# Zero products in front of the turns and products of the query columns, and one fixed PSUM place for them

## Chip, core and metric

One NeuronCore of a Trainium2 chip runs the whole program. The metric is the device time of one execution in microseconds; lower is better. The kernel before was timed three times: median 1874.4 us (1872.93 to 1878.34).

## What is computed

The reference chains three parts: a linear attention, a mixture of eight experts that sends each token to two of them, and a second feed-forward part with a cosine gate. Cut to its core:

```python
q_s = softmax(q over head_dim); k_s = softmax(k over seq)       # (8, 8, 576, 64)
kv  = einsum('bhsd,bhse->bhde', k_s, v)
x   = einsum('bhsd,bhde->bhse', q_s, kv)  -> (4608, 512)
noisy = x @ w_gate + log1p(exp(x @ w_noise)) * noise
top2 experts of each token, weights from a softmax over the two
out[token] += weight * (relu(x[token] @ w1[e]) @ w2[e])
h = out @ w_in ; result = (h * cos(h)) @ w_out
```

## The kernel before

The 4608 tokens are 36 *columns* of 128 tokens: nine for each of four pairs of batches, the ninth of a pair being the last 64 tokens of both.

- **Attention.** 16 steps `s` (batch, half of the heads) load k and v and run `k_stage` (the maximum over the sequence, turned on TensorE, subtracted on GpSimd at L293, exponential on ScalarE at L295) and `kv_stage` (products into `pkv`, L316). Between them stand the query columns.
- **A query column** is `x_unit(n)`: `x_t(n + 1)` turns the queries of the column after it (four transposes, L371, into `pqt`; ScalarE writes their exponential to `qtt`, L373), and `x_mm(n)` multiplies `qtt` with `KVN` into `px` (L387; L392 for a ninth column). VectorE then reads `px` four times: `dx` (L395), `xs` (L398), `lx` (L400), and sums `lx` into the gate logits `lg` (L401). SyncE stores `xs` to `x_d`. `px` is a tile of a PSUM pool with one buffer, so the products of a column wait until VectorE has read those of the column before. `pqt` and `qtt` have two buffers each.
- **Routing.** When columns 0 to 17 are done, `routing(0)` works out on VectorE which token goes to which expert (L444 to L546). Its last steps compare slots (`lo`, `eq`, `bl`, L429), multiply them on TensorE into `ptb` (L532) and write the token lists (`TB` L535, `rit` L539, `idx` L546). Columns 18 to 26 and 27 to 35 have a `routing` of their own.
- **Experts.** With the first lists, GpSimd gathers rows of `x_d` (L621), TensorE turns them (`pt`, L674) and the first three groups of expert 0 (`early_group`) run between the columns from 27 on: `mm1` (`ph`, L753 to L755) and `mm2` (`acc`, L777 to L779). After the columns come the other experts and the last part, over 80% of the time.

The order on each engine is not that of the source. The program is recorded under `schedule_with_timeline_sim=True`: a scheduler takes the recorded instructions and puts those of each engine in an order by its own estimate of their times, within the dependences. `tc.issue_after(x)` adds one dependence, that the instruction comes behind `x` on its engine. The weights of the experts are split on ScalarE and GpSimd (L139, L140) in between.

Of the kernel before, what the change touches and what calls it, by code (L numbers as in the profile page):

```python
# [10 lines left out]
F32 = mybir.dt.float32  # L11
F32R = mybir.dt.float32r
BF16 = mybir.dt.bfloat16
# [8 lines left out]
P = 128  # L22
# [5 lines left out]
def tile_attention_moe_moe2(  # L28
# [14 lines left out]
    nc = tc.nc  # L43
# [25 lines left out]
    consts = ctx.enter_context(tc.tile_pool(name="consts", bufs=1))  # L69
    psa = tc.alloc_tile_pool(name="psa", bufs=1, space=PSUM, side="right")  # L70
# [4 lines left out]
    def ps_at(name, tag, bufs):  # L75

        return psa.tile([P, 512], F32, name=name, tag=tag, bufs=bufs)
# [16 lines left out]
    flag = consts.tile([P, 1 + E], I32, name="flag")  # L94
    ident = consts.tile([P, P], F32, name="ident")
    make_identity(nc, ident)

    def w_pieces(e):

        if e < E:
            a, b = w1[e], w2[e]
        else:
            h = e - E
            a, b = wi_d[:, h * F:(h + 1) * F], wo_d[h * F:(h + 1) * F, :]
        res = []
        for fh in range(2):
            for kc in range(NK):  # L110
                res.append((0, kc, fh, a.rearrange("(p k) f -> k p f", k=NK)[kc, :, fh * 512:(fh + 1) * 512]))
            for f in range(4 * fh, 4 * fh + 4):
                res.append((1, f, 0, b[f * P:(f + 1) * P, :]))
        return res
# [69 lines left out]
    KVN = [at.tile([P, 4, 81], F32, name=f"kvn{i}") for i in range(B)]  # L184
# [172 lines left out]
        nc.gpsimd.tensor_tensor(ql, ql, qm[:, :, None].to_broadcast([P, H, D]), op=ALU.subtract)  # L357

    QTT = {}

    def x_t(n):

        t, c9 = divmod(n, PC)
        pt = ps_at("pqt", "tr", 2)
        for i in range(4):
            if c9 < 8:
                b, c = 2 * t + c9 // 4, c9 % 4
                src = QE[2 * b + i // 2][:, c, 2 * (i % 2):2 * (i % 2) + 2, :]
            else:
                src = QTL[t][:, 2 * i:2 * i + 2, :]  # L370
            nc.tensor.transpose(pt[:, i * P:(i + 1) * P], src.rearrange("p h d -> p (h d)"), ident)  # L371
        qtt = at.tile([P, 4, P], F32, name="qtt", bufs=2)
        behind.append(nc.scalar.activation(qtt, pt.rearrange("p (i s) -> p i s", i=4), AF.Exp))  # L373
        QTT[n] = qtt

    def x_mm(n):
        t, c9 = divmod(n, PC)
        qtt = QTT.pop(n)
        xs = at.tile([P, H, D], F32, name="xs", bufs=4)
        den = at.tile([P, 2, 4], F32, name="dx", bufs=3)  # L380
        px = psa.tile([P, 2, 512], F32, name="px", tag="px", bufs=1)
        for i in range(4):
            for r in range(2):
                rs = slice(64 * r, 64 * r + 64)
                o = px[:, r, i * 81:i * 81 + 81]
                if c9 < 8:
                    nc.tensor.matmul(o, qtt[rs, i, :], KVN[2 * t + c9 // 4][rs, i, :], start=True, stop=True,  # L387
                                     tile_position=(64 * r, 0))
                else:
                    for b2 in range(2):  # L390
                        ts = slice(64 * b2, 64 * b2 + 64)
                        nc.tensor.matmul(o[ts], qtt[rs, i, ts], KVN[2 * t + b2][rs, i, :], start=True, stop=True,  # L392
                                         tile_position=(64 * r, 64 * b2))
        pv = px[:, :, :324].rearrange("p r (i e) -> p r i e", i=4)
        nc.vector.tensor_single_scalar(den, pv[:, :, :, 64], EPS, op=ALU.add)  # L395
        nc.vector.reciprocal(den, den)
        xv = xs.rearrange("p (i r) d -> p r i d", r=2)
        nc.vector.tensor_tensor(xv, pv[:, :, :, :64], den[:, :, :, None].to_broadcast([P, 2, 4, 64]), op=ALU.mult)  # L398
        lx = at.tile([P, 2, 4, 2 * E], F32, name="lx", bufs=2)
        nc.vector.tensor_tensor(lx, pv[:, :, :, 65:], den[:, :, :, None].to_broadcast([P, 2, 4, 2 * E]), op=ALU.mult)  # L400
        nc.vector.tensor_reduce(LG[:, n, :], lx.rearrange("p r i g -> p g (r i)"), axis=AX.X, op=ALU.add)  # L401
        xf = xs.rearrange("p h d -> p (h d)")
        if c9 < 8:
            r0 = (2 * t + c9 // 4) * S
            dst = x_d[r0:r0 + SM, :].rearrange("(p c) m -> p c m", c=4)[:, c9 % 4, :]
            nc.sync.dma_start(dst, xf)
        else:
            for b2 in range(2):
                r0 = (2 * t + b2) * S + SM
                nc.sync.dma_start(x_d[r0:r0 + 64, :], xf[64 * b2:64 * b2 + 64])  # L410
# [179 lines left out]
    def x_unit(n):  # L590
        if n == 0:
            x_t(n)
        if n + 1 < NCOL:
            x_t(n + 1)
        x_mm(n)
        for i, (_, c1) in enumerate(CHUNKS):
            if n + 1 == c1:
                bg.add(routing(i))
# [426 lines left out]
    for n in range(n, NCOL):  # L1025
        t, c9 = divmod(n, PC)
# [57 lines left out]
    with tc.If(over > 0):  # L1084
        with tc.tile_pool(name="gp", bufs=1, reuse_waits="tile") as gp:
            with tc.For_i(0, NT // P, 1) as blk:
# [17 lines left out]
                for e in range(E):  # L1104
# [5 lines left out]
                    for f in range(NF):  # L1110
                        ph = ps_tr("gph")
                        for kc in range(NK):
                            nc.tensor.matmul(ph[:, :P], wa_t[:, kc, f * P:(f + 1) * P], xt[:, kc, :],
                                             start=kc == 0, stop=kc == NK - 1)
# [6 lines left out]
                for h in range(2):  # L1121
# [4 lines left out]
                    for f in range(NF):  # L1126
                        ph = ps_tr("gph")[:, :P]
                        for kc in range(NK):
                            nc.tensor.matmul(ph, wa_t[:, kc, f * P:(f + 1) * P], xt[:, kc, :],
                                             start=kc == 0, stop=kc == NK - 1)  # L1130
                        kk = gp.tile([P, P], F32, name="gkk", bufs=2)
                        r = gp.tile([P, P], F32, name="gr", bufs=2)
                        times_cos(r, kk, ph)
                        nc.tensor.matmul(acc, r, wb_t[:, f, :], start=h == 0 and f == 0,
                                         stop=h == 1 and f == NF - 1)
# [34 lines left out]
```

## Time and profile before

| | |
|---|---|
| median of 3 runs | 1874.4 us (1872.93 to 1878.34) |
| profiled execution: its own time | 1874.38 us |
| its span, first to last instruction | 1872.4 us |
| TensorE busy | 1798.1 us (96%) |
| VectorE, ScalarE, GpSimd busy | 1136.9, 857.8, 452.4 us |
| mean granted TensorE clock | 0.968 of full speed |

The span lacks 2.0 us of the execution's time: what lies before the first and behind the last instruction. TensorE is written PE, its weight loads PEld, VectorE DVE, ScalarE ACT, GpSimd POOL, SyncE's queue SPq. The profile's *PEclk* is the TensorE clock that was granted: 1.00 is 2.4 GHz, 0.50 is 1.2 GHz.

### The profile page before, as it was taken

The numbers are of one execution on the slowest core, as the hardware profiler recorded it, in microseconds if no ns is written. First come the engines' busy times: TensorE is split into PE (matmuls) and PEld (weight loads), VectorE is DVE, ScalarE is ACT, GpSimd is POOL, SyncE is SP. The second block draws the span as 40 slices with busy tenths as digits, with TensorE's granted clock in tenths as the row PEclk, the third lists the DMA queues.
The fourth block names the chain that finished last, engine by engine and source line by source line (L and its number), as shares of the span: only waits on it lengthen the run. The fifth ranks groups of instructions, "written<-read, shape, count | busy, mean of one in ns | idle before, by whom it ended". The sixth has DMA issues, their size and how long they took to land. (4 is left out here: it accounts for less than half of the span.)

```text
span 1872.4 us, 27040 instructions
## 1 busy us (share of the span) xinstructions
PE 1798.1 (96%) x9738; PEld 1525.2 (81%) x9738; DVE 1136.9 (61%) x2138; ACT 857.8 (46%) x1514; POOL 452.4 (24%) x405
## 2 busy tenths in 40 slices
PE   5885999999999999999999999999999999999998
PEld 3674888898988889888888878888888888888886
DVE  4658653686757567575652466565656556565654
ACT  5542223332332323333232376666666666666654
POOL 5556125332313133231323262010101001010000
PEclk7875899999999999999999999999999999999999
DMA  9954335554535455354543352020302021211000
GB/s 265 290 170 121 102 103 189 178 167 142 182 109 161 136 157 173 103 166 130 160 136 111 118 157 68 23 84 7 90 7 84 18 74 29 63 40 40 1 23 24
DMA packets 179775, 206.19 MB, mean 110 GB/s; under 512 B 34224, under 2 KB 121264, under 8 KB 179632
## 3 DMA queue, kind: packets, MB, share of 16 engines
q1 hardware_dynamic: 160704, 152.17, 27.3%
q0 software_dynamic: 12160, 39.86, 7.4%
q10 hardware_dynamic: 6768, 12.32, 1.8%
q8 instruction: 82, 1.34, 0.3%
q14 instruction: 61, 0.50, 0.1%
HBM read 127.06 MB, written 49.43 MB: 94 GB/s over the span
## 5 line engine op out<-in xcount | busy, mean ns | idle before, releaser
L753 PE MATMUL ph<-xh,w1h 128*128 128x512 f32 (+2 forms) x1376 | 489.4, 356 | 3.1 <-DVE r L699 3.1
L755 PE MATMUL ph<-xh,w1l 128*128 128x512 f32 (+2 forms) x1376 | 489.0, 355 | 0.0
L754 PE MATMUL ph<-xl,w1h 128*128 128x512 f32 (+2 forms) x1376 | 488.9, 355 | 0.0
L777 PE MATMUL acc<-w2h,hh 128*128 128x512 f32 x1152 | 451.5, 392 | 1.9 <-ACT hh L765 1.3
L778 PE MATMUL acc<-w2l,hh 128*128 128x512 f32 x1152 | 450.2, 391 | 0.0
L779 PE MATMUL acc<-w2h,hl 128*128 128x512 f32 x1152 | 422.1, 391 | 0.6
L753 PEld LDWEIGHTS ph<-xh,w1h 128*128 128x128 f32 x1376 | 260.1, 189 | 41.0 <-DVE r L699 3.6
L754 PEld LDWEIGHTS ph<-xl,w1h 128*128 128x128 f32 x1376 | 260.1, 189 | 37.6 <-issue 0.8
L755 PEld LDWEIGHTS ph<-xh,w1l 128*128 128x128 f32 x1376 | 259.9, 189 | 31.9
L759 ACT ACTIVATE hh<-ph 128x256 fp32r<-128x256 f32 (+2 forms) x200 | 95.6, 478 | 392.2 <-PE ph L755 387.6
L760 DVE SCALAR_TENSOR_TENSOR hl<-ph,hh 128x256 fp32r<-128x256 f32 (+2 forms) x200 | 108.1, 541 | 247.0 <-ACT hh L759 238.7
L777 PEld LDWEIGHTS acc<-w2h,hh 128*128 128x128 f32 x1152 | 216.5, 188 | 47.6 <-ACT hh L765 3.3
L779 PEld LDWEIGHTS acc<-w2h,hl 128*128 128x128 f32 x1152 | 215.1, 188 | 46.1 <-issue 1.6
L778 PEld LDWEIGHTS acc<-w2l,hh 128*128 128x128 f32 x1152 | 216.5, 188 | 40.4
L699 DVE SCALAR_TENSOR_TENSOR r<-r,ph 128x512 f32<-128x512 f32 x144 | 98.9, 687 | 152.8 <-ACT r L698 152.1
L140 POOL TENSOR_TENSOR w1l<-wst,w1h 128x512 fp32r<-128x512 f32 x80 | 106.1, 1329 | 258.0 <-ACT w1h L139 241.5
L697 ACT ACTIVATE r<-r 128x512 f32<-128x512 f32 x144 | 90.6, 629 | 149.4 <-DVE r L696 149.3
L766 DVE TENSOR_TENSOR hl<-r,hh 128x512 fp32r<-128x512 f32 x144 | 100.5, 698 | 86.2 <-ACT hh L765 86.1
L140 POOL TENSOR_TENSOR w2l<-wst,w2h 128x512 fp32r<-128x512 f32 x80 | 106.6, 1337 | 134.2 <-ACT w2h L139 106.2
L621 POOL DMA_INDIRECT xg<-y_d,SL x36 | 34.7, 965 | 403.8 <-DVE xl L684 368.9
L695 DVE SCALAR_TENSOR_TENSOR r<-kk,ph 128x512 f32<-128x512 f32 x144 | 98.7, 685 | 48.8 <-ACT kk L694 48.6
L621 POOL DMA_INDIRECT xg<-x_d,idx x80 | 76.7, 959 | 193.8 <-DVE xl L684 89.8
(189 smaller groups left out, 2147.8 us busy)
## 6 DMA issues: line engine op xcount, KB each, us to landing
wst<-in_moe_w_dram SPq DMA_DIRECT2D x128, 256.0 KB, 3.3
xl<-xg SPq DMA_DIRECT2D x396, 64.0 KB, 2.3
y_d<-ys ACTq DMA_DIRECT2D x47, 256.0 KB, 2.7
kt<-in_k_dram SPq DMA_DIRECT2D x16, 512.0 KB, 7.2
vt<-in_v_dram SPq DMA_DIRECT2D x16, 512.0 KB, 7.9
qt<-in_q_dram SPq DMA_DIRECT2D x16, 512.0 KB, 8.6
x_d<-xs SPq DMA_DIRECT2D x32, 256.0 KB, 2.8
y_d<-ys SPq DMA_DIRECT2D x29, 256.0 KB, 2.2
```

Of the source, the lines that this page charges most:

```text
L140: nc.gpsimd.tensor_tensor(lo, st, hi.bitcast(F32), op=ALU.subtract)
L621: return nc.gpsimd.indirect_dma_start(out=dst, out_offset=None, in_=src, in_offset=bass.IndirectOffsetOnAxis(ap=ix, axis=0))
L695: nc.vector.scalar_tensor_tensor(r, kk, -C1, ph, op0=ALU.mult, op1=ALU.add)
L699: nc.vector.scalar_tensor_tensor(r, r, 1.0, ph, op0=ALU.subtract, op1=ALU.mult, reverse0=True)
L753: nc.tensor.matmul(ph, w1h[:, kc, fs], g.xh[:, kc, :g.N], start=kc == 0, stop=False)
L754: nc.tensor.matmul(ph, w1h[:, kc, fs], g.xl[:, kc, :g.N], start=False, stop=False)
L755: nc.tensor.matmul(ph, w1l[:, kc, fs], g.xh[:, kc, :g.N], start=False, stop=kc == NK - 1)
L760: after.append(nc.vector.scalar_tensor_tensor(hl, ph, 0.0, hh.bitcast(F32), op0=ALU.max, op1=ALU.subtract))
L766: after.append(nc.vector.tensor_tensor(hl, r, hh.bitcast(F32), op=ALU.subtract))
L777: nc.tensor.matmul(g.acc[m], hh[:, ms], w2h[:, fr, :], start=f == 0, stop=False)
L778: nc.tensor.matmul(g.acc[m], hh[:, ms], w2l[:, fr, :], start=False, stop=False)
L779: nc.tensor.matmul(g.acc[m], hl[:, ms], w2h[:, fr, :], start=False, stop=f == g.nf - 1)
```

## The change

A 128 by 128 tile of zeros is written once. `px` is taken from its pool once, as `PX`, and all columns use it. `fill(k)` issues `k` matmuls of zeros by zeros into columns 384 to 511 of the second half of `PX`, which nothing reads; each is to be issued behind the instruction recorded last in `tail`, which holds the fills, the turns and the products of the columns (not those of ninth columns). Three fills are recorded in front of each column's turns (none for the first column) and five in front of its products: 35 x 3 + 36 x 5 = 285 in all.

```diff
+    zeros = consts.tile([P, P], BF16, name="zeros")
+    nc.vector.memset(zeros, 0.0)
...
+    PX = psa.tile([P, 2, 512], F32, name="px", tag="px", bufs=1)
+    tail = []
+
+    def fill(k):
+
+        if tail:
+            for _ in range(k):
+                with tc.issue_after(tail[-1].ins):
+                    tail.append(nc.tensor.matmul(PX[:, 1, 384:], zeros, zeros, start=True, stop=True))
 
     def x_t(n):
...
+        fill(3)
         for i in range(4):
...
-            nc.tensor.transpose(pt[:, i * P:(i + 1) * P], src.rearrange("p h d -> p (h d)"), ident)
+            tail.append(nc.tensor.transpose(pt[:, i * P:(i + 1) * P], src.rearrange("p h d -> p (h d)"), ident))
...
     def x_mm(n):
...
-        px = psa.tile([P, 2, 512], F32, name="px", tag="px", bufs=1)
+        px = PX
+        fill(5)
...
-                    nc.tensor.matmul(o, qtt[rs, i, :], KVN[2 * t + c9 // 4][rs, i, :], start=True, stop=True,
-                                     tile_position=(64 * r, 0))
+                    tail.append(nc.tensor.matmul(o, qtt[rs, i, :], KVN[2 * t + c9 // 4][rs, i, :], start=True, stop=True,
+                                                 tile_position=(64 * r, 0)))
```

The scheduler makes a new order of all engines from this. Three places of it matter below. Line numbers of the changed kernel are higher: L371, L387, L392, L532, L674 and L753 are L383, L400, L405, L545, L687 and L766, and a fill is L370.

**First place: PE, from the end of the last slot products (`ptb`) to the first turn of gathered rows (`pt`).** Before, two columns (24 and 25) stand between them:

```order
L532 MATMUL ptb<-bl,lo_2094 128x160
L371 MATMUL pqt<-ident,qe 128x128 x4
L387 MATMUL px<-kvn_99,qtt 128x81 x8
L371 MATMUL pqt<-ident,qe 128x128 x4
L387 MATMUL px<-kvn_99,qtt 128x81 x8
L674 MATMUL pt<-ident,xg_1685 128x128 x4
```

With the change, where "..." at a pair of `zeros` rows stands for seven more such pairs (the queries of the ninth column, `qtl`, are turned here too):

```order
L545 MATMUL ptb<-bl,lo_2272 128x160
L383 MATMUL pqt<-ident,qtl 128x128 x4
L370 LDWEIGHTS zeros
L370 MATMUL px<-zeros 128x128
...
L400 MATMUL px<-kvn_101,qtt 128x81 x8
L383 MATMUL pqt<-ident,qe 128x128 x4
...
L400 MATMUL px<-kvn_101,qtt 128x81 x8
L383 MATMUL pqt<-ident,qe 128x128 x4
...
L400 MATMUL px<-kvn_101,qtt 128x81 x8
L687 MATMUL pt<-ident,xg_1814 128x128 x4
```

Three columns (23 to 25) stand there now, and the eight fills of a column stand together, directly in front of its products and behind the turns. The first of the eight waits for VectorE's reads of the column before, as the products did.

**Second place: DVE, from the last slot comparison (`bl`) to the first list (`idx`).** Before:

```order
L429 TENSOR_TENSOR bl<-eq_2096,tx 128x480 x2
L395 TENSOR_SCALAR dx<-px 128x8
L396 RECIPROCAL dx<-dx 128x8
L535 COPY TB<-ptb 128x160
L398 TENSOR_TENSOR xs<-px,dx 128x2x4x64
L400 TENSOR_TENSOR lx<-px,dx 128x128
L539 SCALAR_TENSOR_TENSOR rit<-TB 128x80
L401 TENSOR_REDUCE lg<-lx 128x16
L546 CAST idx_73<-rit 128x4
```

With the change:

```order
L442 TENSOR_TENSOR bl<-eq_2274,tx 128x480 x2
L408 TENSOR_SCALAR dx<-px 128x8
L409 RECIPROCAL dx<-dx 128x8
L411 TENSOR_TENSOR xs<-px,dx 128x2x4x64
L413 TENSOR_TENSOR lx<-px,dx 128x128
L414 TENSOR_REDUCE lg<-lx 128x16
L548 COPY TB<-ptb 128x160
L552 SCALAR_TENSOR_TENSOR rit<-TB 128x80
L559 CAST idx_73<-rit 128x4
```

The column read here is 23 before and 22 now: one column's reads have moved behind the list.

**Third place: PE, from the last key and value products (`pkv`) on.** With the change the products of four columns (14 to 17) stand behind them, before those of three (15 to 17):

```order
L318 MATMUL pkv<-vtl_108,ktz_95 64x65 x2
L383 MATMUL pqt<-ident,qtl 128x128 x4
L370 LDWEIGHTS zeros
L370 MATMUL px<-zeros 128x128
...
L400 MATMUL px<-kvn_99,qtt 128x81 x8
L334 MATMUL pkt<-ident,kvn_103 64x128 x4
```

The loads of the queries of the second ninth column (`qtl`, two DMAs on SyncE's queue) also stand together there now; before, a store of `x_d` stood between them. Behind the last column's products PE's order is the same but for a few rows.

## Rows read from the trace of the kernel before

**Rows 1.** The page: busy time by engine, and the 40 slices.
```profile
PE 1798.1 (96%) x9738; PEld 1525.2 (81%) x9738; DVE 1136.9 (61%) x2138; ACT 857.8 (46%) x1514; POOL 452.4 (24%) x405
...
PE   5885999999999999999999999999999999999998
...
PEclk7875899999999999999999999999999999999999
```

**Rows 2.** Stretches: length, busy us (x count) by engine, PEclk, DMA share, GB/s.
```profile
0.00:105.00 105.00, 70.22 (x878) 56.77 (x879) 62.35 (x163) 56.54 (x91) 65.00 (x73) 0.78 1.03 281
105.00:140.60 35.60, 30.95 (x398) 25.57 (x396) 20.98 (x60) 15.00 (x27) 13.96 (x9) 0.79 0.38 124
140.60:183.20 42.60, 24.79 (x193) 20.91 (x192) 38.81 (x95) 11.87 (x24) 25.70 (x19) 0.58 0.38 114
195.10:198.50 3.40, 3.40 (x18) 3.40 (x17) 3.13 (x15) 0.98 (x2) 0.00 (x0) 0.50 0.27 105
198.60:237.60 39.00, 39.00 (x356) 33.89 (x354) 25.51 (x86) 10.43 (x22) 2.72 (x4) 1.00 0.20 67
237.60:1872.40 1634.80, 1620.08 (x7829) 1376.73 (x7825) 978.60 (x1702) 757.45 (x1336) 337.31 (x293) 1.00 0.33 99
```

**Rows 3.** Stretches at one clock each, from 96 us to 198.5 us.
```profile
96.20:109.80 13.60, 11.66 (x122) 10.09 (x122) 10.60 (x30) 7.35 (x11) 7.89 (x6) 0.50 0.94 312
116.70:126.90 10.20, 10.20 (x98) 8.67 (x99) 4.38 (x15) 4.88 (x8) 7.64 (x6) 0.50 0.13 51
...
161.10:174.60 13.50, 6.49 (x44) 5.55 (x45) 13.47 (x26) 1.63 (x3) 7.00 (x5) 0.50 0.22 65
174.70:178.10 3.40, 1.03 (x14) 0.85 (x14) 3.40 (x8) 0.00 (x0) 1.44 (x2) 1.00 0.00 0
178.20:198.50 20.30, 17.70 (x133) 15.23 (x132) 14.74 (x47) 8.24 (x17) 10.20 (x9) 0.50 0.68 213
```

**Rows 4.** Timeline, PE, 167 to 196 us: start, length, what, [idle before <- releaser].
```profile
167.89 0.98 PE L532 MATMUL ptb<-bl,lo 128*128 128x160 bf16 x6 [7.90 <-DVE bl L429]
...
176.77 0.59 PE L532 MATMUL ptb<-bl,lo 128*128 128x160 bf16 x6 [2.12 <-DVE bl L429]
...
181.53 2.00 PE L387 MATMUL px<-kvn,qtt 64*128 64x81 f32 x16 [0.30 <-DVE lx L400]
184.56 1.11 PE L371 MATMUL pqt<-ident,qe 128*128 128x128 f32 x4 [1.03 <-ACT qtt L373]
185.61 2.00 PE L387 MATMUL px<-kvn,qtt 64*128 64x81 f32 x16
...
195.08 0.58 PE L753 MATMUL ph<-xh,w1h 128*128 128x256 f32 x1
195.46 0.41 PE L754 MATMUL ph<-xl,w1h 128*128 128x256 f32 x1
195.67 0.41 PE L755 MATMUL ph<-xh,w1l 128*128 128x256 f32 x1
```

**Rows 5.** Timeline, 131 to 134 us, at the full clock: a column's loop.
```profile
131.66 1.12 PE L387 MATMUL px<-kvn,qtt 64*128 64x81 f32 x16
...
132.89 0.60 ACT L373 ACTIVATE qtt<-pqt 128x512 f32<-128x512 f32 x1 [2.45 <-PE px L387]
...
133.54 0.66 PE L371 MATMUL pqt<-ident,qe 128*128 128x128 f32 x4 [0.20 <-ACT qtt L373]
```

**Rows 6.** Timeline, DVE, 133 to 136 us: column 15's reads and a wait.
```profile
133.03 0.20 DVE L396 RECIPROCAL dx<-dx 128x8 f32<-128x8 f32 x1
133.27 0.69 DVE L398 TENSOR_TENSOR xs<-px,dx 128x512 f32<-128x512 f32 x1
133.88 0.28 DVE L400 TENSOR_TENSOR lx<-px,dx 128x128 f32<-128x128 f32 x1
136.04 0.69 DVE L356 TENSOR_REDUCE qml<-qtl 128x8 f32<-128x512 f32 x1 [1.88 <-DMA qtl<-in_q_dram]
```

**Rows 7.** Timeline, DVE, 178 to 181 us: the last slot comparison and what follows.
```profile
178.22 0.36 DVE L401 TENSOR_REDUCE lg<-lx 128x16 f32<-128x128 f32 x1
178.50 0.71 DVE L429 TENSOR_TENSOR bl<-eq,tx 128x480 bf16<-128x480 bf16 x2
179.34 0.17 DVE L395 TENSOR_SCALAR dx<-px 128x8 f32<-128x8 f32 x1
```

**Rows 8.** Timeline, PE, 205 us, at the full clock.
```profile
205.46 0.28 PE L755 MATMUL ph<-xh,w1l 128*128 128x256 f32 x1
205.58 0.28 PE L753 MATMUL ph<-xh,w1h 128*128 128x256 f32 x1
```

**Rows 9.** Timeline, DVE, 142 us: `routing(0)` begins on DVE.
```profile
142.10 0.31 DVE L444 TENSOR_SCALAR rs<-rt 128x144 f32<-128x144 f32 x1 [1.13 <-ACT rt L438]
```

## The prediction, made before the change was run

> **What bounds the kernel now.** The page comes first: TensorE is busy for 96% of the span, but in the first five of the 40 slices, some 234 us, PEclk is 5 to 8 tenths, and full afterwards [rows 1]. So the stretches come next [rows 2]. From 198.6 us on PE has work without a gap: 39.0 of 39.0 us busy up to 237.6 us, and 1620 of 1635 us from there to the end. Whatever is put on PE behind 198.6 us is paid in full, and whatever makes PE reach that state earlier is won in full, since the order of PE behind the columns stays as it was. All that the clock can give lies before 198.6 us. There the limits change from stretch to stretch:
>
> - Up to 105 us the DMA engines are full (share 1.03): loads of q, k and v. PE at double speed would wait for them.
> - From 105 to 140.6 us PE is busy for 30.95 of 35.60 us, at a mean clock of 0.79; it waits in part for the chain of the key steps over ACT and POOL.
> - From 140.6 to 183.2 us DVE is busy for 38.81 of 42.60 us (`routing(0)`), PE for only 24.79. PE's clock falls, and it costs nothing.
> - From there to 198.5 us PE is the limit again, all at half clock: 17.70 of 20.30 us busy, counted from 178.2 us [rows 3]. Here a column goes round one loop: its products (2.00 us), ACT's `qtt`, the next turn (1.11 us), the next products, 4.08 us from one product start to the next [rows 4]. At the full clock the same loop is 132.89 - 131.66 = 1.23 us to ACT's start, 0.65 us to the turn and 0.66 us for it, 2.54 us [rows 5].
>
> So the question is at which clock PE passes 178 to 198 us, and what the fills cost there and behind.
>
> **The price of a fill.** The trace has no product of 128 bf16 columns by itself. The nearest rows: a 256-column product follows the one before after 0.12 us at the full clock [rows 8] and 0.21 us at half [rows 4], so 128 columns are 0.06 and 0.105 us. From above: six `ptb` products of 160 bf16 columns, each with its own weight load, take 0.59 us in all at full clock and 0.98 us at half, drain included [rows 4], so at most 0.10 and 0.16 us each. `ptb` is more like a fill, but its group counts one drain that a fill does not pay, as products follow it; I take the lower ends: eight fills are 0.48 us at the full clock and 0.85 us at half, at most 0.8 and 1.3 us. Below the lower ends nothing, since the columns have to be streamed.
>
> The first of the eight waits for DVE's reads of the column before, and all stand behind the turns. So a fill never runs in the gap in which PE waits for DVE; it comes when the wait is over, in front of the products.
>
> **Up to 105 us, and 140.6 to 183.2 us: 0.** Cover: the DMA engines in the one, DVE in the other. Without DVE's cover the five columns of the routing stretch would cost 5 x 0.85 = 4.3 us. The memset of the zeros is one DVE instruction at the start, under the loads.
>
> **105 to 140.6 us: +0.4 us.** The last key products are followed by four columns now instead of three, one loop more with its fills: 2.54 + 0.48 = 3.0 us. The other three pay 3 x 0.48 = 1.4 us. Won back: the wait of 1.88 us of DVE for the second half of the ninth column's queries [rows 6], whose two loads no longer have a store between them; and some of the 10.20 us of unbroken work at half clock [rows 3], which is 5.1 us at full. A column with its fills is denser work than one without, and I take half, 2.6 us, since ACT and POOL set a part of this chain. 3.0 + 1.4 - 1.9 - 2.6 = -0.1; 0.5 us for fills of earlier columns that are not covered makes +0.4. Ends: if the clock were full in both half stretches from 96 us on (11.66 and 10.20 us of work, half of it 10.9 us) less nine sets of fills (4.3 us), -6.6 us; if it changed nowhere and all nine sets were paid at half clock, +7.7 us. The two lie about equally far, and the value is near their middle.
>
> **178 to 195 us: -2.6 us.** One column's reads have moved behind the list. They are 0.17 + 0.20 + 0.69 + 0.28 + 0.36 = 1.7 us [rows 6, 7]. So the last slot comparison, which ended at 178.50 + 0.71 = 179.2 us, ends at 177.5 us, and DVE has read column 22 (0.17 + 0.20 + 0.69 + 0.28) at 178.9 us. Then PE does five columns, 23 to 27, before the first expert product. At the full clock: 178.9 + 0.48 for the fills, four loops of 2.54 + 0.48 = 3.02 us, and 1.12 us of products, ends at 192.6 us. Before, the first expert product started at 195.08 us [rows 4]: 2.5 to 2.6 us won. At half clock: 178.9 + 0.85 + 4 x (4.08 + 0.85) + 2.00 = 201.5 us, 6.4 us lost.
>
> I take the full clock. Before, the `ptb` products were followed by a rise for one stretch, 174.7 to 178.1 us, and the clock fell again behind a stretch in which PE was busy for only 1.03 of 3.40 us [rows 3]. With the change the columns of that stretch bring eight dense products each, and the columns behind follow without the waits that DVE's routing work made.
>
> **195.1 to 198.5 us: -1.7 us.** Expert products at half clock, PE busy 3.40 of 3.40 us [rows 2]. At the full clock they take half. If the clock is still low there: 0.
>
> **198.6 to 237.6 us: +3.8 us.** Eight columns (28 to 35) among expert products, PE never idle [rows 2]: 8 x 0.48 us. At the upper price 6.4 us, and not less than 3.8 us.
>
> **Behind 237.6 us: 0**, as the order is the same.
>
> The sum: 0.4 - 2.6 - 1.7 + 3.8 = -0.1 us. The profiled execution took 1874.38 us (span 1872.4 us), the median of the runs is 1874.4 us, so nothing has to be carried over: **1874.3 us**, no change.
>
> The Trainium skill, page "TensorE: Matmul & The Clock Gate", table under "Why this matters for your kernels", speaks against the change: pauses of TensorE between bursts of matmuls put it back to the low clock, and the remedy is to have no pauses. The trace agrees: after a wait of 7.90 us for DVE PE found half clock [rows 3, 4]. By it alone the fills, which stand behind the waits, would hold nothing up, and the sum would be that of the second rival.
>
> **Rivals.**
>
> *The clock stays up from 96 us on.* Columns with eight dense products each might keep the clock up through both half stretches and let routing start earlier. For it: PE is busy for 10.20 of 10.20 us in the second [rows 3], so its length is PE's own. Against it: DVE, ACT and POOL have their part in the loop. Its price is the lower end above, -6.6 instead of +0.4 us: 1874.4 - 6.6 - 2.6 - 1.7 + 3.8 = 1867.3 us. The same page, section "Part 4: PE-mode transpose", says that transposes don't count as a busy engine in the way that matmuls do. By it the fills are what the column loop lacked, and this rival would be the likeliest; no row here separates turns from products.
>
> *Five columns at half clock.* One mechanism: the column loop at half clock is PE 2.00 + 1.11 us and a pause for ACT (1.03 us [rows 4]) in every round; if the fills lengthen the round without lifting the clock, columns 23 to 27 end at 201.5 us. It decides if PEclk is 0.50 after 180 us. For it: 17.70 of 20.30 us busy did not lift it before [rows 3]. Against it: the fills would be about a sixth of a round, all of it dense. Then 1874.4 + 0.4 + 6.4 + 3.8 = 1885.0 us.
>
> *The fills do not do what they are for.* The clock keeps its old course, the moved column evens out, and the columns before 198.6 us hide their fills. Only the eight dense columns pay: 1874.4 + 3.8 = 1878.2 us.
>
> **How the numbers follow.** A measurement of this kernel can tell about 0.3%, 5.6 us, from no change. Forecast 0.42 (1874.3), first rival 0.25 (1867.3), second 0.20 (1885.0), third 0.13 (1878.2). The first rival is faster by over 0.3% nearly always, the second slower; forecast and third are within it but for their edges. Faster 0.25, same 0.53, slower 0.22. The range reaches from the first rival's value to a little under the second's, 1867 to 1884 us, which leaves out the farther halves of both, some 0.2.
>
> **What would show it.** Right: PEclk at 1.00 from 178 us on; the first `ph` product near 192 to 193 us; columns 3.0 us apart there; eight `zeros` products in about 0.48 us behind the turns; PE without a gap and eight columns 0.5 us longer from 198 us on. Wrong: PEclk at 0.50 between 180 and 195 us and columns 4.9 us apart (second rival); routing's first step on DVE, at 142.10 us before [rows 9], earlier by over 4 us (first rival); or `zeros` products far from 0.06 us.

## The result: 17 us slower

The changed kernel took 1891.3 us (median of 4 runs, 1887.62 to 1896.23) beside 1873.8 us (4 runs) of the kernel before: ratio 1.0091, 95% interval 1.0074 to 1.0109, some 14 to 20 us slower. The profiled execution, the slowest of the four, took 1896.23 us, with a span of 1894.4 us against 1872.4 us.

From the page of the changed kernel, the lines that answer to [rows 1]:

```profile
PE 1816.3 (96%) x10023; PEld 1544.7 (82%) x10023; DVE 1139.5 (60%) x2139; ACT 857.1 (45%) x1514; POOL 453.9 (24%) x405
...
PE   5786999999999999999999999999999999999998
...
PEclk8885799999999999999999999999999999999999
```

TensorE has 285 instructions more and 18.2 us more of work, and the span is 22 us longer. PEclk is higher in the first and the third slice, the same 5 in the fourth, and lower in the fifth.

For the rest the program is cut at four events: routing's first step on DVE, the first list (`idx`), the first expert product (`ph`), the products of the last column. The stretches between them, before:

```profile
105.00:142.10 37.10, 32.34 (x412) 26.99 (x410) 21.35 (x61) 16.00 (x30) 15.43 (x11) 0.78 0.38 123
142.10:182.20 40.10, 22.40 (x172) 18.50 (x172) 37.53 (x94) 10.87 (x21) 23.34 (x18) 0.59 0.37 112
182.20:195.10 12.90, 10.60 (x95) 8.85 (x93) 8.29 (x22) 5.52 (x12) 8.60 (x8) 0.50 0.80 244
195.10:236.80 41.70, 41.70 (x339) 36.71 (x337) 28.50 (x99) 11.03 (x23) 2.72 (x4) 0.96 0.19 65
```

And with the change (columns as in [rows 2]; the last line is all that is behind the last column):

```profile
105.00:146.90 41.90, 34.86 (x518) 29.78 (x518) 24.85 (x69) 18.13 (x33) 20.00 (x14) 0.86 0.36 112
146.90:185.90 39.00, 24.39 (x193) 21.72 (x194) 37.41 (x88) 8.79 (x18) 23.15 (x16) 0.54 0.31 96
185.90:205.20 19.30, 16.94 (x154) 14.83 (x151) 8.54 (x25) 7.37 (x15) 10.27 (x9) 0.54 0.71 213
205.20:254.70 49.50, 47.25 (x400) 41.77 (x398) 28.65 (x100) 10.36 (x24) 2.70 (x4) 0.93 0.19 66
254.70:1894.40 1639.70, 1622.55 (x7859) 1378.77 (x7857) 980.04 (x1704) 757.90 (x1338) 337.39 (x293) 1.00 0.33 98
```

Routing starts 4.8 us later, its own stretch is 1.1 us shorter, from the list to the first expert product it takes 6.4 us more, from there to the last column 7.8 us more. That is 17.9 us. The rest, 1639.7 against 1635.6 us, differs by 4 us; over the traces below with the same order there it lies between 1633 and 1640 us, so I do not read it.

The stretches at one clock each, from 115 us:

```profile
115.10:138.80 23.70, 20.86 (x350) 17.89 (x349) 12.67 (x35) 9.17 (x17) 10.96 (x7) 1.00 0.34 106
...
180.00:203.70 23.70, 17.53 (x144) 15.62 (x145) 13.19 (x34) 6.34 (x12) 13.44 (x12) 0.50 0.55 168
203.90:210.50 6.60, 5.20 (x61) 4.71 (x58) 5.77 (x24) 1.86 (x6) 0.00 (x0) 1.00 0.27 79
210.70:217.30 6.60, 5.82 (x33) 5.21 (x33) 4.46 (x20) 1.05 (x3) 0.77 (x2) 0.50 0.12 43
```

Two things differ from [rows 3]. From 115 to 139 us the clock is full now, where it was half for 10 us. But the column loop in front of the first expert product runs at half clock as before, for longer, and the clock falls once more amid the expert products, from 210.6 to 217.4 us. In that loop, on PE:

```profile
186.40 2.00 PE L400 MATMUL px<-kvn,qtt 64*128 64x81 f32 x16
189.25 1.09 PE L383 MATMUL pqt<-ident,qe 128*128 128x128 f32 x4 [0.85 <-ACT qtt L385]
190.13 1.06 PE L370 MATMUL px<-zeros 128*128 128x128 bf16 x8
191.12 2.00 PE L400 MATMUL px<-kvn,qtt 64*128 64x81 f32 x16
```

A round is 191.12 - 186.40 = 4.72 us. The pause for ACT is there as before (0.85 us; 1.03 us in [rows 4]), and the eight fills put products 0.99 us later. The forecast's price for a round at half clock was 4.93 us.

Where the fills stand in PE's waits is seen over the stretch up to routing, grouped by what PE did (busy us, mean ns, then the idle time in front of it and who ended it):

```profile
L400 PE MATMUL px<-kvn,qtt 64*128 64x81 f32 x258 | 21.6, 314 | 0.0
L370 PE MATMUL px<-zeros 128*128 128x128 bf16 x152 | 14.8, 249 | 9.7 <-DVE lx L413 9.6
L383 PE MATMUL pqt<-ident,qe 128*128 128x128 f32 x80 | 14.3, 307 | 5.1 <-ACT qtt L385 5.1
```

The products themselves wait for nothing any more: the fills wait in their place for DVE's reads of the column before, and then run. So they lie on a chain of their own, since `px` is one place: DVE reads a column (three reads of `px`: `dx`, `xs` and `lx`), eight fills, the next products, DVE reads those. The trace of one round at the full clock:

```profile
137.54 0.28 DVE L413 TENSOR_TENSOR lx<-px,dx 128x128 f32<-128x128 f32 x1
...
137.87 0.61 PE L370 MATMUL px<-zeros 128*128 128x128 bf16 x8 [1.09 <-DVE lx L413]
138.41 1.58 PE L400 MATMUL px<-kvn,qtt 64*128 64x81 f32 x16
140.03 0.17 DVE L408 TENSOR_SCALAR dx<-px 128x8 f32<-128x8 f32 x1 [1.81 <-PE px L400]
```

PE stands still for 1.09 us until `lx` is done, then does the fills, 0.54 us to the products' start, and DVE, which waits 1.81 us, gets its column that much later.

### The profile page after: what moved, and what is told of

Its sections match the earlier page's. It is cut to its first block, busy times and chain, and to the rows that moved or that the text cites. A ratio compares the mean times of both kernels' runs of the same rounds, so it can differ in the third digit from the quotient of the medians.

```text
span 1894.4 us, 27576 instructions
## 1 busy us (share of the span) xinstructions
PE 1816.3 (96%) x10023; PEld 1544.7 (82%) x10023; DVE 1139.5 (60%) x2139; ACT 857.1 (45%) x1514; POOL 453.9 (24%) x405
## 5 line engine op out<-in xcount | busy, mean ns | idle before, releaser
L766 PE MATMUL ph<-xh,w1h 128*128 128x512 f32 (+2 forms) x1376 | 489.7, 356 | 3.5 <-DVE r L712 3.5
L766 PEld LDWEIGHTS ph<-xh,w1h 128*128 128x128 f32 x1376 | 260.1, 189 | 41.5 <-DVE r L712 3.9
```

What stands on the lines that cost most here:

```text
L766: nc.tensor.matmul(ph, w1h[:, kc, fs], g.xh[:, kc, :g.N], start=kc == 0, stop=False)
```

## The experiments

All ratios below are to the kernel before in runs on the same chip, which took 1875 to 1878 us there; 0.1% is 1.9 us. Unless said otherwise an edit is made to the changed kernel, and the fills change nothing of what is computed.

### The fixed place alone (e1_px)

```diff
-        if tail:
+        if False:
             for _ in range(k):
```

> The one fixed PSUM place for px alone, no fills; TensorE's order is that of the kernel before. The kernel before is 1873.8 us, the changed one 1891.3 us. My theory (the fills are paid for in PE's time, and the place is free): 1873 to 1875 us, last column at 236.8 us as before. Rival (the fixed place costs, by a wait of the products for the place): up to the whole loss, 1878 to 1891 us, with the products of px starting later behind VectorE's lg than before. Rival (the scheduler's new order costs): 1874 us too, as the order is the old one.

Measured: 0.9996 (0.9983 to 1.0009), last column at 238.0 us. No cost of the place can be told from noise.

### Fills in a part of the columns (e2_late, e3_mid, e4_early)

```diff
+        if 28 <= n < 36:
             fill(3)
...
+        if 28 <= n < 36:
             fill(5)
```

and the same with columns 18 to 27 and 0 to 17.

> Fills in columns 28 to 35 alone, where PE has work without a gap; the order before them is the old one. My theory: eight columns by the 0.54 us that eight fills took in the changed kernel at the full clock = 4.3 us, and nothing else: 1878 us (1877 to 1880), last column near 241 us. Rival (the fixed place, or the order ahead of the first expert product, holds the loss): within 1 us of the kernel before, 1874 us. If the half-clock stretch that the changed kernel had amid the expert products (210.6 to 217.4 us) is made by these fills, it is seen here too and adds 3.4 us: 1881 us.

Measured: 1.0019 (1.0009 to 1.0029), 3.6 us, last column at 241.9 us, the clock full from 199 us on. So the dense columns cost what eight fills take, 8 x 0.54 = 4.3 us or a little less, and alone, in this trace, they do not pull the clock down.

> Fills in columns 18 to 27 alone. My theory: the columns beside routing's work on VectorE hide them, the columns from there to the first expert product are a loop at half clock, and pay 1.0 us each, with one column more in front of the first expert product if the scheduler makes that order: 1877 to 1884 us, clock 0.50 from 180 to 200 us. Rival (fills lift the clock there, and the loss lies elsewhere): clock 1.00 from 180 us on and 1868 to 1872 us. Rival (the fixed place costs): as much as the run without any fill.

Measured: 0.9988 (0.9977 to 0.9999). My theory missed. Four columns stand in front of the first expert product, not five, and the clock comes up in the middle of them:

```profile
174.00:187.40 13.40, 9.29 (x70) 8.66 (x72) 12.09 (x25) 1.75 (x3) 6.53 (x6) 0.50 0.29 99
187.60:196.60 9.00, 7.02 (x107) 5.91 (x105) 6.14 (x17) 5.35 (x11) 6.97 (x7) 1.00 0.81 232
```

With that the fills there pay for themselves, as the forecast had it, and no more.

> Fills in columns 0 to 17 alone. My theory: routing's first step on VectorE (142.10 us before, 146.93 us with the change) comes 4 to 5 us later, through the column loops behind the last key products, and the columns behind are as before: 1877 to 1880 us. Rival (the loss of the first part is the scheduler's order, one column more behind the last pkv product, and not the fills' time): the order is the same as in the changed kernel up to there, so only the run with narrow fills tells that; but the clock tells something: full from 115 to 139 us as in the changed kernel if the fills lift it.

Measured: 1.0016 (1.0006 to 1.0026), 3.0 us. The expectation wanted routing 4 to 5 us later; its trace, of the fastest of the twelve executions, has it at 143.2 us. The ten traces with no fills in columns 0 to 17 have it at 140.3 to 143.5 us, so this one shows no delay. The four traces with fills behind as well and the same order up to there (the changed kernel, e7, e8, e11) have it at 145.3 to 149.3 us.

The three parts make 1.0019 - 0.0012 + 0.0016 = 1.0023, 4.3 us. The whole is 17 us, so 13 us are lost by the parts together.

### Two parts together (e8_to27, e9_from18)

> Fills in columns 0 to 27: the early and the middle ones together, which apart gave 1.0016 and 0.9988 of the kernel before. Alone, each left four columns between the last ptb product and the first ph product in the recorded order; together they leave five, as in the changed kernel. My theory (the five columns at half clock are what is paid; the fills as such cost little ahead of 200 us): first ph product at 203 to 206 us as in the changed kernel, last column near 249 us, 1884 to 1888 us. Rival (the fills' parts add up, and what the changed kernel loses beyond them is made behind 200 us): first ph near 198 us, 1875 to 1878 us.

> Fills in columns 18 to 35: the middle and the late ones together, four columns between the last ptb and the first ph product. My theory (five columns at half clock are what is paid): the sum of the parts, 0.9988 and 1.0019, 1875 to 1879 us, first ph near 197 us, last column near 242 us. Rival (middle and late fills disturb each other: gaps of PE behind the first expert products, and a fall of the clock there): last column over 248 us, 1884 us or more.

Measured: 1.0051 (1.0038 to 1.0065) for columns 0 to 27, 1.0006 (0.9997 to 1.0015) for 18 to 35. The second pair adds up. The first does not: 9.6 us instead of 0.8. In the recorded orders the difference is the one that the expectation names, five columns instead of four between the last slot products and the first expert product, and the trace has it there:

```profile
184.50:203.30 18.80, 16.43 (x152) 14.12 (x149) 8.05 (x25) 7.20 (x15) 10.27 (x9) 0.57 0.68 213
```

18.8 us from the list to the first expert product, against 11.3 and 12.7 us in the two runs with one part each.

### The fifth column taken back (e11_four)

```diff
-                    nc.tensor.matmul(pt[:, :2 * NTB], lo1[:, j, :, i], ...)
+                    with tc.issue_after(LAST[23]) if c + 3 == 18 and j + i == 0 else contextlib.nullcontext():
+                        nc.tensor.matmul(pt[:, :2 * NTB], lo1[:, j, :, i], ...)
```

`LAST[23]` is the last product of column 23.

> All fills of the changed kernel, and one dependence more: the last three products into ptb are issued behind the products of column 23. So four columns stand between the last ptb and the first ph product, as before the change, instead of five. My theory (the fifth column at half clock is half of the loss): the columns 0 to 27 without it are worth about 9 us, as between the run with fills in columns 0 to 27 and the sum of its two parts; 1880 to 1884 us, first ph product near 197 us. Rival (the number of columns is a symptom; PE's pauses and the fills cost the same in any order): 1888 us or more, first ph at 203 us or later.

Measured: 1.0048 (1.0031 to 1.0066), 8 us less than the changed kernel's 1.0091. (Its median, 1887.6 us, stands beside 1877.7 us of the kernel before; at 1873.8 us the ratio gives 1882.8 us, where the expectation had 1880 to 1884.) The size came out, the place only in part: the stretch from the list to the first expert product is 12.4 us, as before the change, but the list itself is 4 us later, since the slot products now wait for column 23 with its fills. The first expert product comes at 202.4 us, not near 197. The other half of the gain is behind it: 46.1 instead of 49.5 us to the last column, with the clock full throughout. The two stretches:

```profile
190.00:202.40 12.40, 9.46 (x122) 8.01 (x121) 7.47 (x19) 5.73 (x12) 8.75 (x8) 0.86 0.72 219
202.40:248.50 46.10, 44.29 (x400) 39.17 (x398) 28.52 (x100) 10.59 (x24) 2.72 (x4) 1.00 0.23 80
```

PEclk is 0.86 in the loop, where it was 0.54 with five columns. So the 8 us belong to the fifth column together with the clock, and this run does not part the two. The 4.7 us between 1.0048 and the parts' 1.0023 are tied to no single cause by any run.

### What the fills are made of (e7_ones, e5_tiny)

```diff
-    nc.vector.memset(zeros, 0.0)
+    nc.vector.memset(zeros, 1.0)
```

> The tile holds ones where the change has zeros: the same instructions in the same order, and the fills' result is still read by nobody. My theory (the data of the fills do not matter to the clock or the time): as the changed kernel, 1888 to 1894 us, half clock from about 180 to 203 us. Rival (products of zeros do not hold the clock up as real products do): full clock in the column loop before the first ph product and from 97 us on, 1867 to 1880 us.

```diff
-                    tail.append(nc.tensor.matmul(PX[:, 1, 384:], zeros, zeros, start=True, stop=True))
+                    tail.append(nc.tensor.matmul(PX[:, 1, 384:386], zeros, zeros[:, :2], start=True, stop=True))
```

> All 285 fills, each 2 columns wide instead of 128: the same count of instructions, weight loads included, and hardly any streaming. The scheduler leaves four columns between the last ptb and the first ph product here, not five. My theory (the fills' time in the loop, and five columns at half clock): most of the loss is gone, 1874 to 1880 us; eight such fills take under 0.3 us where the full ones took 0.61 us. Rival (instructions and weight loads as such, or the scheduler's new order ahead of the columns, cost): over 1886 us, and eight fills as long as the full ones.

Measured: 1.0091 (1.0075 to 1.0107) with ones, the zeros' own figure, and half clock from 180.8 to 204.7 us. So ones or zeros make no difference, and this second trace of the same order has the late half-clock stretch too (214.9 to 218.3 us). With narrow fills 1.0009 (0.9995 to 1.0022), no difference that can be told. Eight of them, at the full clock:

```profile
125.17 0.34 PE L370 MATMUL px<-zeros 128*128 128x2 bf16 x8
125.44 1.12 PE L400 MATMUL px<-kvn,qtt 64*128 64x81 f32 x16
```

They put the products 0.27 us later, half as much as the wide ones. The number of instructions as such is not what costs. How much of the rest is the fills' width and how much the fifth column, this run cannot say, as its order has four.

### Fewer columns in front of the first expert product (e13_three, e14_mid3)

```diff
-            dbg.step(2)
+            dbg.step(8)
```

in the loop over the columns, at column 26; e13 without fills, e14 with fills in columns 18 to 27.

> No fills, the fixed place, and the first expert group recorded six steps earlier, so that three columns instead of four stand between the last ptb and the first ph product. My theory read the other way (each column there costs a round at half clock, and behind the first ph product 1.8 us): 4.1 - 1.8 = 2.3 us gained, 1871 to 1873 us, first ph near 191 us. Rival (the gathered rows, landing near 188.5 us and with the turn's copies behind them, set the first ph product): no gain, 1874 us, first ph over 194 us.

> Fills in columns 18 to 27 alone (0.9988 by itself), and the first expert group recorded six steps earlier: three columns in front of the first ph product. My theory: both gains add up, as far as the clock is full in the loop there: 1868 to 1872 us. Rival (the gathered rows set the first ph product, or the earlier expert work starves column 27 and what waits for it, the second routing): 1873 us or more.

Measured: 1.0015 (1.0004 to 1.0026) and 1.0005 (0.9995 to 1.0016), both as their rivals had it. The first expert product came at 196.2 us where e1 had 194.5, and at 194.7 us where e3 had 196.7; from it to the last column it took 50.1 and 50.8 us instead of 43.4 and 41.1, with more of the experts' work among the columns. To have fewer columns in the loop is not worth anything by itself.

### The same fills in another place (e12_gap, e17_gap2, e18_gap12, e16_gap9, e15_gapall)

```diff
     def x_t(n):
         pt = ps_at("pqt", "tr", 2)
-        fill(3)
+        for _ in range(8 if 18 <= n < 28 else 0):
+            nc.tensor.matmul(pt[:, :P], zeros, zeros, start=True, stop=True)
...
     def x_mm(n):
-        fill(5)
```

All eight go into the place of the turns, which the turns then overwrite, and are no longer tied by `issue_after`; e16 has columns 9 to 27, e15 columns 1 to 35 (280 fills), e18 twelve fills.

> Eight fills a column, for the turns of columns 18 to 27 alone, written into the place of the turns (which the turns then overwrite) instead of the place of the products. So they do not wait for VectorE's reads of the column before and can run in PE's pause. Four columns stay between the last ptb and the first ph product. My theory (fills behind the wait lengthen the loop, fills in the pause do not): PE without a gap in the column loop, full clock from about 188 us on or earlier, column products no more than 4.2 us apart even where the clock is half; 1868 to 1873 us. Rival (the pause is not what keeps the clock low): half clock to 198 us as before, and 1874 us or more.

> The kernel of e12_gap again, for a second trace. My theory (fills in the pause bring the clock up, when they come at the right moment): the runs lie at 1867 to 1872 us as five of the six did, and a trace of such a run has full clock in a part of the loop from 178 to 198 us, with the first ph product at 189 to 193 us. Rival (the gain is not made there): first ph at 196 us again, and the time won behind it.

> Twelve fills instead of eight for the turns of columns 18 to 27, in the place of the turns. My theory (at half clock eight fills take 1.0 us, as long as the pause; twelve take 1.5 us and fill it more surely, but lengthen a round by 0.5 us where the clock stays low): 0.994 to 0.997, clock up earlier than in e12_gap. Rival (more fills only lengthen the loop): 0.998 or more, half clock to 198 us.

> Eight fills for each column's turns, in the place of the turns, columns 9 to 27. My theory: the columns 9 to 17 hide them in the pause too and their clock is full more often, so routing starts no later than 143 us: 0.993 to 0.997. Rival (fills in columns 9 to 17 stand in the way of the key steps' products, which have no pause): routing starts at 145 us or later, 0.998 or more.

> Eight fills for each column's turns, columns 1 to 35, written into the place of the turns: 280 fills where the changed kernel has 285, but in PE's pause instead of behind its wait. Four columns in front of the first ph product. My theory (their place behind the wait is what costs ahead of the first ph product): as the run with them in columns 18 to 27, 0.9955, plus 8 x 0.54 = 4.3 us in the dense columns (0.23%) and up to 3 us for the early ones: 0.998 to 1.000, 1870 to 1875 us where the kernel before is at 1875; no gap of PE and no half clock behind 200 us. Rival (their number, or the new order, costs): 1.005 or more, 1884 us or more.

Measured: e12 0.9955 (0.9940 to 0.9970), the same kernel again as e17 0.9967 (0.9954 to 0.9980), e18 0.9970 (0.9958 to 0.9981), e16 0.9955 (0.9941 to 0.9969), e15 0.9982 (0.9972 to 0.9992). All are faster than both kernels, the best by 6 to 11 us than the kernel before. The nearest pair for the place is eight fills in columns 18 to 27, with four columns in front of the first expert product each time: 0.9988 in the place of the products (e3), 0.9955 and 0.9967 in that of the turns (e12, e17), 4 to 6 us better. e15 has the changed kernel's number of fills and is 1.0091 - 0.9982 = 1.1%, 20 us, faster than it. Its stretches:

```profile
105.00:139.30 34.30, 28.88 (x456) 25.00 (x455) 20.01 (x56) 14.03 (x26) 15.69 (x12) 0.89 0.41 127
139.30:180.60 41.30, 25.27 (x222) 22.44 (x221) 39.10 (x94) 10.90 (x22) 24.68 (x18) 0.62 0.35 109
180.60:190.50 9.90, 7.70 (x100) 6.62 (x98) 5.27 (x16) 4.55 (x8) 7.72 (x7) 0.87 0.88 264
190.50:234.40 43.90, 43.90 (x405) 38.59 (x402) 29.03 (x103) 11.66 (x27) 2.73 (x4) 1.00 0.24 84
```

Against the changed kernel routing starts 7.6 us earlier, the loop in front of the first expert product is 9.4 us shorter, and the columns behind are 5.6 us shorter, with no idle time and no fall of the clock. (The first expert product stands alone in front of the products of the loop's last column here; the others follow from 191.9 us on.) Up to routing its waits are these:

```profile
L400 PE MATMUL px<-kvn,qtt 64*128 64x81 f32 x260 | 20.8, 302 | 4.3 <-DVE lx L413 4.2
L377 PE MATMUL pqt<-zeros 128*128 128x128 bf16 x168 | 15.7, 245 | 7.9 <-ACT qtt L386 7.9
L384 PE MATMUL pqt<-ident,qe 128*128 128x128 f32 x80 | 15.4, 315 | 0.0
```

The fills wait for ACT now, as the turns did, and the products for DVE: a fill runs between the two waits, while DVE is still reading. One round:

```profile
129.37 0.61 PE L377 MATMUL pqt<-zeros 128*128 128x128 bf16 x8 [0.75 <-ACT qtt L386]
129.81 0.61 PE L384 MATMUL pqt<-ident,qe 128*128 128x128 f32 x4
...
130.86 0.28 DVE L413 TENSOR_TENSOR lx<-px,dx 128x128 f32<-128x128 f32 x1
...
131.19 1.11 PE L400 MATMUL px<-kvn,qtt 64*128 64x81 f32 x14 [0.77 <-DVE lx L413]
```

Nothing stands between `lx` and the products, and 0.77 us of PE's wait for `lx` are still left.

Two parts of my expectation fell. The pause for ACT is not filled, as the place of the turns waits for ACT too. And in e12, e16, e17 and e18 the loop in front of the first expert product has fills in its first round only, as the turns behind belong to columns past 27. In e12's trace it ran at half clock to the end, 4.08 us a round; but that execution took 1877.7 us, no less than the kernel before, and the other five took 1867 to 1872 us. So it does not show how the fast ones go. The second trace of this kernel (e17, 1870.9 us) has full clock in a part of the loop. From the list to the first expert product, e12 and then e17:

```profile
183.70:196.00 12.30, 10.38 (x91) 8.56 (x89) 7.50 (x21) 5.58 (x12) 7.71 (x7) 0.50 0.83 262
182.00:193.10 11.10, 9.17 (x92) 7.62 (x90) 7.54 (x22) 5.57 (x12) 7.72 (x7) 0.65 0.85 263
```

That is what e17 was expected to show. In e18's trace (1867.6 us) PEclk is 0.55 there, so the gain does not hang on this loop alone. In e16's trace it is seen earlier:

```profile
105.00:139.20 34.20, 27.62 (x444) 23.90 (x444) 20.03 (x58) 14.66 (x29) 15.54 (x11) 0.90 0.34 110
139.20:179.40 40.20, 23.97 (x224) 21.44 (x222) 39.00 (x93) 10.84 (x21) 24.53 (x18) 0.71 0.36 110
179.40:191.40 12.00, 10.31 (x99) 8.42 (x98) 7.52 (x21) 5.68 (x12) 7.73 (x7) 0.64 0.83 264
```

PEclk is 0.90 and 0.71 in the first two stretches, where it was 0.78 and 0.59, and routing starts 2.9 us earlier. That is thin: 139.2 us here and 139.3 us in e15 lie only 1 us outside the 140.3 to 143.5 us of the ten traces with no fills in columns 0 to 17, and by the times columns 9 to 17 add nothing (0.9955 beside 0.9955 and 0.9967). So the place is worth its time by the runs; where in the program it is won is not shown.

## Why the prediction was wrong

The failed step is the choice at *178 to 195 us*: "I take the full clock". It was half, and the second rival is what happened: five columns in front of the first expert product, rounds of 4.72, 4.66, 4.67 and 3.73 us priced at 4.93. I gave that 0.20 and 1885.0 us. By the traces that rival is short by 4.4 us up to routing and by 4.0 us behind the first expert product. By the steps:

- *The price of a fill* (0.48 us for eight at the full clock, 0.85 at half): 0.54 and 0.99 us to the products' start. Right in kind; measured, it is 13 to 16% more.
- *Up to 105 us, 0*: not separated here; the early columns' whole effect is in the next step.
- *105 to 140.6 us, +0.4 us*: +4.8 us in the pair of traces, 3.0 us (1.1 to 4.9) by e4's time alone; inside the bounds, far from the value. The clock did come up in the profiled trace (0.86 for 0.78; 0.77 in that of e7, with the same order), as the first rival had it, but four rounds behind the last key products took 4.0 to 4.2 us instead of 3.0, two of them at the full clock. The price of 2.54 us for a round there was mis-sized: it follows ACT's chain [rows 5] and leaves out what else stands in these rounds. Before the change too, the rounds from 131.66 us on take 3.04 and 3.69 us at the full clock. In the second PE waits for `lx`, which on DVE stands behind the wait for `qtl` [rows 6]:

```profile
134.70 1.12 PE L387 MATMUL px<-kvn,qtt 64*128 64x81 f32 x16
...
138.39 0.80 PE L392 MATMUL px<-kvn,qtt 64*64 64x81 f32 x32 [1.15 <-DVE lx L400]
```

With the change the wait for `qtl` was not won back:

```profile
135.62 0.69 DVE L358 TENSOR_REDUCE qml<-qtl 128x8 f32<-128x512 f32 x1 [1.97 <-DMA qtl<-in_q_dram]
```

- *178 to 195 us, -2.6 us*: the stretch from the list to the first expert product is 6.4 us longer. e8 and e11 tie 8 to 9 us to the five columns, of which a part is in the late columns. That the clock can come up in this loop is shown by e3, with the same fills and one column less: it is full from 187.5 us on, in e9 from 187.3 us and in e11 from 190.0 us, but for 3.4 us. With four columns and no fills of these columns it came up at 193.2 us or later (the kernel before, e1, e2, e4). I had taken what was possible for what is likely; why it stayed at half with five columns, in all three traces, stays open. The Trainium skill, page "TensorE: Matmul & The Clock Gate", table under "Why this matters for your kernels", has the low clock follow from pauses between bursts. The traces do not settle whether that is the cause here. The fills left the pause for ACT where it was (0.85 us of each round), and the clock at half; but e15's round above, with pauses of 0.75 and 0.77 us, ran at the full clock, which fell at 132.0 us. And in the prediction's example the clock fell at 161.0 us, 1.0 us into the wait of 7.90 us [rows 3, 4].
- *195.1 to 198.5 us, -1.7 us*: right in direction. The first twelve products into `ph` start 0.12 us apart but for the first pair, at the full clock: 1.5 us instead of 2.7, so 1.2 us are won.
- *198.6 to 237.6 us, +3.8 us*: 3.6 us by e2 alone, so the price was right. In the changed kernel this term and the one before it make +7.8 us together, where the forecast had +2.1. "PE never idle" no longer held: PE waits twice, and the clock falls between the two waits, at 210.6 us.

```profile
209.21 0.61 PE L370 MATMUL px<-zeros 128*128 128x128 bf16 x8 [1.40 <-DVE lx L413]
...
211.49 0.22 PE L489 MATMUL pr<-M,ltri 128*128 128x72 bf16 x1 [0.85 <-DVE M L442]
```

1.4 and 0.9 us of waiting and half of the 6.8 us at half clock make 5.7 us at most beside the fills. e11, which has the same fills there and full clock, lost 4.4 us of the 7.8. What brings the late fall stays open. It does not go with the five columns: e8 has five, PE waits for 2.3 us behind the first expert product, and the clock stays full; e1, without any fill, and e5 have four, and 3.4 us of half clock amid the expert products (from 200.1 and 200.2 us on). In e8:

```profile
203.30:246.20 42.90, 40.57 (x339) 35.26 (x337) 29.33 (x102) 11.01 (x24) 2.72 (x4) 1.00 0.19 61
```

- *Behind, 0*: nothing that stands out of the scatter of the traces.

The forecast added up terms by stretch. "All stand behind the turns", and in front of the products, was in it as a remark on the pauses. What it means for the chain through `px`, whose single place DVE must have read first, was not priced: fills there delay DVE's next column in every round. e15 shows that the place, with the order that comes with it and without `issue_after`, and not the number of fills, is worth 20 us. Beside e11, without the fifth column, 1.0048 - 0.9982 = 0.66%, 12 us, are left; in them are the 4 us by which e11's own dependence delays the list. No run tells the place from the missing `issue_after`.

## What to carry to other kernels

Work put in to hold TensorE's clock up must not stand between the end of a wait and the work that was waited for: look at which buffer it writes, as that decides which wait it inherits, and whether it lies on the loop that sets the pace. Some 280 products cost 17 us in one place and gained 3 us in another. And with a scheduler in between, effects of parts need not add: compare the orders, and price the place at which they differ.

## What the runs showed of the hardware

- Fills of ones and of zeros gave the same ratio (1.0091 both) and the same half clock in the loop (179.9 to 203.8 us and 180.8 to 204.7 us). Other values were not tried.
- A product of 128x128 weights by 2 columns takes 0.27 / 8 = 0.034 us at the full clock, one by 128 columns 0.54 / 8 = 0.068 us: a product with 126 columns less still takes half as long.
- The same kernel run twice (e12 and e17) had the loop in front of the first expert product at half clock throughout in one trace, and at full clock for a part of it in the other (mean 0.50 and 0.65), with the first expert product at 196.0 and 193.1 us; the two executions took 1877.7 and 1870.9 us. A single trace is thin evidence on the clock; the comparisons of times are what the conclusions rest on.
